# FNet block with SwiGLU, one core: hidden matrices loaded by 64 rows, modulation added up on VectorE, list of steps ranked anew, branch hint at the end

## The chip, the core and the metric

The kernel runs on one core of one Trainium2 chip. The metric is the device time in microseconds of one execution; "the time" of a kernel is the median over runs. A core has TensorE (PE, with its weight loads shown apart as PEld), VectorE (DVE), ScalarE (ACT), GpSimd (POOL) and SyncE (SP). Each engine works through its own list of instructions in the order in which the program issued them. SP issues most transfers, GpSimd those that gather rows or add to what is in memory.

## The reference

```
x    = A_x                                       # [1, 2048, 512]
mod  = (silu(c) @ w_mod) -> sa, ca, ga, sb, cb, gb   # six vectors of 512
h    = layernorm(x) * (1 + ca) + sa
a, b = h @ dft_hid_re.T, h @ dft_hid_im.T        # transform along the 512
y    = dft_seq_re @ a - dft_seq_im @ b           # transform along the 2048
x    = x + ga * y
h    = layernorm(x) * (1 + cb) + sb
x    = x + gb * ((silu(h @ w1) * (h @ w3)) @ w2) # 512 -> 1792 -> 512
```

All is float32. The kernel multiplies most matrices by splitting each into a high part and a low part (three products) in a faster matmul format, and it uses the symmetries of the transform matrices.

## The kernel before, in words

**Stages.** The program has three stages: the hidden transform of the first normalised rows, the sequence transform, and the SwiGLU part. The edits sit in the first stage, in what comes before it, and at the end of the third.

**Before the first stage.** SP issues in this order: `c`; the two halves of x block 0 (`load_x`, L205 and L207); the four blocks of the modulation matrix that give `ca` and `sa` (`load_wm`, L216, 512 KB each; v = 1 is `ca`, v = 0 is `sa`); x block 1; the hidden transform's matrices (`load_hid`, L226, real and imaginary part for each of four column groups dt); x blocks 2 and 3. Meanwhile `keep_warm` runs dummy matmuls (L270), x block 0 is normalised (L424 to L445) and turned by TensorE (L460). Then `mod_sum` multiplies the modulation matrix by silu(c) with matmuls of one column (L292); each (v, h) is a group of 8 matmuls, all in one PSUM bank, and after each group VectorE moves or adds the four columns into `mod1` (L302, L93).

**The first stage.** It goes over NK = 8 blocks k, each of two sides of 128 rows. The steps of a block are: statistics, root, inverse, scale (`stats`, `root`, `inverse`, `scale`), transposes (`turn`), modulation of the turned rows (`mod`, writes `hm`, L476 on ScalarE or L478 on VectorE), sums and differences of the two sides (`sum`, writes `hs`), their high and low parts (`hh`, `hl`), the second side's copy (`h1`), four products with the hidden matrices (`prod`, L524), the odd half (`odd`), the mirrored product (`mirror`, L560), the product with the differences (`diff`, L541), and the copies of the results out of PSUM as high and low parts (`uh`, `us`, `ul`, `up`, `ush`, `ulh`). The hidden matrices themselves are prepared per dt: high part on ScalarE (`wh`), low part on VectorE (`wl`), differences on GpSimd (`wd`, L390, L395), negated copies on ScalarE (`wn`).

**The order.** These steps are tasks with a rank, a list of needs and a planned duration for each engine that can do them. `arrange` keeps a clock for each engine and, again and again, issues among the tasks that could begin within 0.3 us of the earliest the one with the lowest rank. Ranks are offsets from `k * PACE`. The lines with `at(...)` tell the planner at what time the loads and the modulation are supposed to be there. The planner's result is only an order of issue: on the chip an engine waits at the head of its list for whatever that instruction needs.

**After it.** `seq_unit` (L714) begins the sequence transform as soon as the last row block's products are there. In the third stage `down` computes an output block; the last eight `y` in the list are the last eight such blocks.

**The end.** A flag that the kernel computed says whether the general kernel has to run instead. Every engine reads it and branches (L2340).

Of the kernel before, what the change touches and what calls it, by code (L numbers as in the profile page):

```python
# [12 lines left out]
OP = mybir.AluOpType  # L13
# [29 lines left out]
def folded(nc, pools, c, cp, wmr, wmc, x, xt, ctr, cti, wdr, wdi, w1, w3, w2, out):  # L43
# [8 lines left out]
    consts, small, big, psum, dram = pools  # L52
# [169 lines left out]
    def load_hid(dt):  # L222
        i, par = HD[dt]
        raw_w[dt] = take(F32, "w")
        for m, w in enumerate((wdr, wdi)):
            nc.sync.dma_start(raw_w[dt][:, m, :], w[i][par::2].rearrange("r q n -> q r n"))  # L226
# [4 lines left out]
    load_wm(0)  # L231
    load_x(1)
    for dt in range(ND):
        load_hid(dt)
# [51 lines left out]
    mod_acc = bank(6)[:, : 4 * ND].rearrange("p (a b) -> p a b", b=ND)  # L286

    def mod_sum(v, h):

        for dt in range(ND):  # L290
            for n in range(2):
                nc.tensor.matmul(  # L292
                    mod_acc[:, 2 * v + h, dt : dt + 1],
                    hid_cols(wm[v, h][:, n, :], dt),
                    sc[:, 2 * h + n : 2 * h + n + 1],
                    start=n == 0,
                    stop=n == 1,
                )
        give(wm.pop((v, h)))

    def mod_half(v):
        nc.vector.tensor_scalar(mod1[:, v, :], mod_acc[:, 2 * v, :], float(v), None, op0=OP.add)  # L302

    def mod_end(v):
        plus(mod1[:, v, :], mod_acc[:, 2 * v + 1, :], mod1[:, v, :])
# [993 lines left out]
    def last_steps(k):  # L1299
        r = k * PACE  # L1300
        wait = [f"us{k}", f"ul{k}", f"mirror{k}.1", *[f"wd{dt}" for dt in range(ND)]]
        task(f"diff{k}", r + 7, wait, lambda: hid_difference(k), PE=0.96)
        task(f"up{k}", r + 8, [f"diff{k}", f"odd{k}"], lambda: high_columns(k, 0), DVE=0.61)
        task(f"ush{k}", r + 12, [f"up{k}"], lambda: high_columns(k, 1), ACT=0.55)
        task(f"ulh{k}", r + 14, [f"ush{k}"], lambda: high_columns(k, 2), DVE=0.61)

    PACE = 7.5
# [21 lines left out]
    at(12.0, "turn0.0", "turn0.1")  # L1329
    at(13.2, "x1")  # L1330
    for dt in range(ND):
        at(14.5 + 1.6 * dt, f"w{dt}")
    for k in range(2, 4):
        at(21.0 + 1.8 * (k - 2), f"x{k}")
    for engine in clear:
        clear[engine] = 13.2
# [3 lines left out]
    for dt in range(ND):  # L1340
        task(f"wh{dt}", -8 + 2 * dt, [f"w{dt}"], lambda dt=dt: w_highs(dt), ACT=0.8)
        task(f"wl{dt}", -6 + 2 * dt, [f"wh{dt}"], lambda dt=dt: w_lows(dt), DVE=0.8)
        task(f"wd{dt}", -6 + 2 * dt, [f"wl{dt}"], lambda dt=dt: differ_w(dt), POOL=3.0)
# [5 lines left out]
    task("zz", 2 * PACE, [], clear_z, ACT=1.0)  # L1349
    for k in range(NK):  # L1350
        r = k * PACE
        both = [f"{k}.0", f"{k}.1"]
        if k:
            for s in range(2):
                task(
                    f"stats{k}.{s}", r - 13 + s / 2, [f"x{k}"],
                    lambda k=k, s=s: norm_stats(k, s), DVE=0.85,
                )
            task(
                f"root{k}", r - 12.2, [f"stats{n}" for n in both], lambda k=k: norm_root(k), ACT=0.2  # L1360
            )
            task(f"inverse{k}", r - 12, [f"root{k}"], lambda k=k: norm_inverse(k), DVE=0.4)
            free_banks = [f"mod{k - 2}.{dt}" for dt in range(ND)] if k > 1 else []
            for s in range(2):
                task(
                    f"scale{k}.{s}", r - 11.5 + s, [f"inverse{k}"],
                    lambda e, k=k, s=s: norm_scale(k, s, e), ACT=0.63, DVE=0.54,
                )
                task(
                    f"turn{k}.{s}", r - 11 + s, [f"scale{k}.{s}", *free_banks],  # L1370
                    lambda k=k, s=s: turn_rows(k, s), PE=0.5,
                )
        for dt in range(ND):
# [12 lines left out]
        task(f"h1{k}", r - 5, sums_done, lambda k=k: mirror_part(k), ACT=0.55)
        for dt in range(ND):
            needs = [f"hl{k}", f"wl{dt}"]
            if dt == 0 and k > 1:
                needs.append(f"up{k - 2}")  # L1390
            if dt:
                needs.append(f"prod{k}.{dt - 1}")
            if dt == 2:
                needs.append(f"odd{k}")
            task(f"prod{k}.{dt}", r + 2 * dt, needs, lambda k=k, dt=dt: hid_product(k, dt), PE=0.72 + 0.23 * (dt == 0))
        task(f"odd{k}", r + 1, [f"prod{k}.1"], lambda k=k: hid_odd(k), ACT=0.53)
        for n in range(2):
            needs = [f"h1{k}", *[f"wl{dt}" for dt in range(ND)], *[f"wn{dt}" for dt in range(2)]]
            if k:
                needs.append(f"uh{k - 1}.{n}")  # L1400
            if k == NK // 2:
                needs += [f"wd{dt}" for dt in range(ND)]
            if n:
                needs.append(f"mirror{k}.0")
            us_pe = 0.91 if k != NK // 2 else 2.7 + 0.9 * n
            task(f"mirror{k}.{n}", r + 3 + n, needs, lambda k=k, n=n: hid_mirror(k, n), PE=us_pe)
            task(
                f"uh{k}.{n}", r + 4 + n, [f"mirror{k}.{n}", "zz"] if k == NK // 2 else
                [f"mirror{k}.{n}"], lambda k=k, n=n: mirror_highs(k, n), ACT=0.53,
            )  # L1410
        task(f"us{k}", r + 5, [f"prod{k}.3"], lambda k=k: low_columns(k, 0), ACT=0.53)
        task(f"ul{k}", r + 6, [f"us{k}"], lambda k=k: low_columns(k, 1), DVE=0.61)
# [167 lines left out]
    for i in range(len(items)):  # L1580
# [723 lines left out]
def fnet_swiglu_block(  # L2304
# [28 lines left out]
    bad = folded(nc, (*pools, dram), *args)  # L2333
# [6 lines left out]
    with tc.If(flag != 0, preferred_fallthrough_block=False):  # L2340
# [57 lines left out]
```

## Time and profile before

| | us |
|---|---|
| median of 3 runs | 749.0 |
| lowest, highest run | 748.25, 749.11 |
| the profiled execution: its time, its span | 749.39, 747.5 |
| busy in the span: PE, DVE, ACT, POOL | 700.2, 548.8, 426.4, 127.6 |
| first modulated row (L476) begins | 23.40 |
| last load of a hidden matrix used (L87) | 55.87 |
| first matmul of the sequence stage (L714) begins | 123.3 |
| last computing instruction ends | 738.04 |

The profile is one execution. Its page gives the busy time of each engine, the span in 40 slices with each engine's busy tenths, the clock granted to TensorE and the transfer rate, and the chain of work that ended last. Rows in order of time read: start, duration, engine, line, operation, output from inputs, shape, count, and in brackets how long the engine had been idle and what ended it. "SPq" rows are transfers as SP issues them: their duration is the issue, not the landing.

### The profile page before, as it was taken

Reading aid. Unit: us, or ns where it says so; the run is one execution under the profiler, and the core shown is the slowest. Engines: PE = TensorE matmul, PEld = TensorE weight load, DVE = VectorE, ACT = ScalarE, POOL = GpSimd, SP = SyncE. Lnnn points to the kernel's source line nnn. Section 1 sums busy time; section 2 is a strip of 40 time slices with the busy share of each in tenths; the row PEclk is TensorE's granted clock in tenths of the full one; section 3 lists DMA queues with packets and bytes.
Section 4 is the critical chain, followed back from the end, with each engine's and each line's share of the span. In section 5 each row is a group of like instructions: output and inputs, shape, how many; then the busy total and the mean of one; then the engine's idle time right before and its main releaser. Section 6 shows DMA issues by size and latency. Waiting matters only on the chain.

```text
span 747.5 us, 8859 instructions
## 1 busy us (share of the span) xinstructions
PE 700.2 (94%) x3140; PEld 572.2 (77%) x3140; DVE 548.8 (73%) x873; ACT 426.4 (57%) x694; POOL 127.6 (17%) x147
## 2 busy tenths in 40 slices
PE   8618989999999999989999999999999999999994
PEld 5407878888888888868788788777888888888783
DVE  2318887899889997767998888789566655665662
ACT  2208877753554456563667867687655655656430
POOL 1212204634424500010011011001100101001000
PEclk8558999999999999999999999999999999999998
DMA  5142305997859753054186655745947548456503
GB/s 186 51 132 81 114 1 169 347 316 246 284 183 323 248 180 140 28 90 81 57 206 119 181 94 133 142 84 113 232 135 169 118 79 177 69 122 128 155 0 117
DMA packets 37716, 108.92 MB, mean 146 GB/s; under 512 B 4640, under 2 KB 4896, under 8 KB 37664
## 3 DMA queue, kind: packets, MB, share of 16 engines
q0 software_dynamic: 12352, 43.00, 27.9%
q1 hardware_dynamic: 25312, 65.29, 25.9%
q8 instruction: 26, 0.43, 0.2%
q14 instruction: 26, 0.21, 0.1%
HBM read 76.81 MB, written 33.55 MB: 148 GB/s over the span
## 4 chain that ended last, share of the span: by engine, by line
PE 70%; DVE 7%; issue 6%; ACT 6%; SPq 4%; DMA 4%; POOL 0%; POOLq 0%; ACTq 0%; DVEq 0%
PE bank L100 45%; PE bank L714 24%; SPq L226 4%; DMA w<-in_wdi 3%; DMA sum<-y 1%; DVE hm L478 1%; DVE hl L90 1%; ACT xc L858 1%; ACT y L308 1%; ACT hm L476 1%; DVE hs L93 1%; DVE st L424 0%; PE bank L560 0%; POOL sum L1110 0%; DVE ul L90 0%
## 5 line engine op out<-in xcount | busy, mean ns | idle before, releaser
L100 PE MATMUL bank<-hf,w2h 128*128 128x512 f32 (+1 forms) x452 | 140.8, 391 | 0.5 <-ACT y L308 0.2
L1110 POOL DMA_DIRECT2D sum<-y x48 | 41.1, 855 | 390.5 <-ACT y L308 373.0
L100 PEld LDWEIGHTS bank<-hf,w2h 128*128 128x128 f32 x452 | 84.3, 188 | 22.4 <-DVE hf L90 3.5
L100 PE MATMUL bank<-hf,w2l 128*128 128x512 f32 (+1 forms) x226 | 87.6, 388 | 0.0
L308 ACT ACTIVATE y<-bank,gb 128x512 f32<-128x512 f32 x96 | 64.9, 682 | 18.6 <-PE bank L100 18.2
L87 ACT ACTIVATE hf<-v 128x512 fp32r<-128x512 f32 x56 | 35.3, 630 | 67.1 <-DVE v L96 62.5
L93 DVE TENSOR_TENSOR v<-bank,x 128x512 f32<-128x512 f32 x36 | 24.7, 686 | 34.8 <-PE bank L100 34.8
L714 PE MATMUL bank<-d,us 128*128 128x512 f32 x128 | 49.9, 390 | 0.0
L714 PE MATMUL bank<-bh,us 128*128 128x512 f32 x128 | 49.9, 390 | 0.0
L714 PE MATMUL bank<-bh,ul 128*128 128x512 f32 x128 | 49.8, 389 | 0.0
L714 PE MATMUL bank<-l,us 128*128 128x512 f32 x128 | 49.8, 389 | 0.0
L714 PE MATMUL bank<-d,uh 128*128 128x512 f32 x128 | 49.8, 389 | 0.0
L714 PE MATMUL bank<-l,uh 128*128 128x512 f32 x128 | 49.8, 389 | 0.0
L100 PEld LDWEIGHTS bank<-hf,w2l 128*128 128x128 f32 x226 | 42.4, 188 | 8.3
L170 POOL DMA_INDIRECT re<-in_ctr,mirror x32 | 36.4, 1137 | 71.9 <-DVE ul L90 35.8
L93 DVE TENSOR_TENSOR x<-bank,x 128x512 f32<-128x512 f32 x36 | 24.8, 688 | 32.3 <-PE bank L100 28.7
L90 DVE TENSOR_TENSOR hf<-v,hf 128x512 fp32r<-128x512 f32 x56 | 38.5, 687 | 12.2 <-ACT hf L87 12.1
L87 ACT ACTIVATE x<-bank 128x512 f32<-128x512 f32 x72 | 41.4, 586 | 7.2 <-PE bank L100 6.5
L1188 ACT ACTIVATE v<-v 128x512 f32<-128x512 f32 x36 | 22.7, 632 | 39.0 <-DVE v L93 39.0
L170 POOL DMA_INDIRECT im<-in_cti,mirror x32 | 34.3, 1073 | 36.4 <-PE bank L714 10.8
L524 PE MATMUL bank<-wu,hh 128*128 128x256 f32 x128 | 27.1, 306 | 13.7 <-ACT ho L87 10.4
L524 PEld LDWEIGHTS bank<-wu,hh 128*128 128x128 f32 x128 | 22.4, 204 | 17.8 <-ACT ho L87 11.8
(241 smaller groups left out, 1807.8 us busy)
## 6 DMA issues: line engine op xcount, KB each, us to landing
sum<-y POOLq DMA_DIRECT2D x48, 512.0 KB
w<-in_w SPq DMA_DIRECT2D x42, 512.0 KB
re<-in_ctr SPq DMA_DIRECT2D x32, 256.0 KB
im<-in_cti SPq DMA_DIRECT2D x32, 256.0 KB
wmc<-in_wmc SPq DMA_DIRECT2D x8, 512.0 KB
xr<-in_xt SPq DMA_DIRECT2D x8, 512.0 KB
sum<-xr SPq DMA_DIRECT2D x8, 512.0 KB
x<-in_x SPq DMA_DIRECT2D x12, 256.0 KB
```

The source lines that it names most:

```text
L87: nc.scalar.activation(dst, src, AF.Copy, scale=scale)
L90: nc.vector.tensor_tensor(out=dst, in0=a, in1=b, op=OP.subtract)
L93: nc.vector.tensor_tensor(out=dst, in0=a, in1=b, op=OP.add)
L100: nc.tensor.matmul(acc, lhs[a], rhs[b], start=first and n == 0, stop=last and n == len(PASSES) - 1, skip_group_check=more,)
L170: nc.gpsimd.indirect_dma_start(dst, None, rows, bass.IndirectOffsetOnAxis(ap=at, axis=0))
L226: nc.sync.dma_start(raw_w[dt][:, m, :], w[i][par::2].rearrange("r q n -> q r n"))
L308: nc.scalar.activation(dst, src, AF.Identity, scale=by)
L476: nc.scalar.activation(dst, src, AF.Identity, bias=sa, scale=ca1)
L524: nc.tensor.matmul(halves(hb[k])[:, m, :], sides((hh, hl)[a][k])[:, dt, m, :], wu[dt][:, b, m, :], start=False, stop=dt % 2 == 1 and n == ...
L714: nc.tensor.matmul(acc[what, e], lhs, rhs, start=begin and i == 0, stop=(end or (turn and what == "x")) and i == len(terms) - 1, skip_grou ...
L1110: nc.gpsimd.dma_start(sums[t, d // 2], y, accum_op=OP.add)
L1188: behind(k != 0 or q == 0, lambda: nc.scalar.activation(v, src, AF.Silu))
```

## The change

1. **Loads.** `load_hid` issued one transfer for a matrix's part, with the destination's 128 partitions written as 2 groups of 64. Now it issues one for each group: 16 transfers of 128 KB and not 8 of 256 KB. The first column group's are issued ahead of x block 1.
2. **Modulation.** For each v, ScalarE scales one block by silu(c), VectorE adds the other three onto it (each multiplied by its own column of silu(c)), and TensorE sums over partitions with 4 matmuls for each v: 8 and not 32. There are two `keep_warm` matmuls between the two groups and one after them. `zz` is cleared here and no longer in the list.
3. **List.** Ranks stand in a table, `PACE` is 7.15 and not 7.5, the planner's times for the loads and some planned durations are others.
4. **End.** The branch is laid out without a preferred block, and each engine gets a hint ahead of the fourth last output block that the branch is likely taken.

```diff
-            nc.sync.dma_start(raw_w[dt][:, m, :], w[i][par::2].rearrange("r q n -> q r n"))
+            for q in range(2):
+                nc.sync.dma_start(raw_w[dt][q * 64 : (q + 1) * 64, m, :], w[i][par::2, q])
...
     load_wm(0)
+    load_hid(0)
     load_x(1)
-    for dt in range(ND):
+    for dt in range(1, ND):
         load_hid(dt)
...
-    mod_acc = bank(6)[:, : 4 * ND].rearrange("p (a b) -> p a b", b=ND)
-    def mod_sum(v, h):
+    mod_acc = bank(6)
+    def mod_scale(v, h):
+        w, own = wm[v, 0][:, 0, :], wm[v, h]
+        if h == 0:
+            copy_by(w, w, sc[:, 0:1])
+        for n in range(1 - h, 2):
+            nc.vector.scalar_tensor_tensor(
+                w, own[:, n, :], sc[:, 2 * h + n : 2 * h + n + 1], w, op0=OP.mult, op1=OP.add
+            )
+    def mod_sum(v):
         for dt in range(ND):
-            for n in range(2):
-                nc.tensor.matmul(
-                    mod_acc[:, 2 * v + h, dt : dt + 1],
-                    hid_cols(wm[v, h][:, n, :], dt),
-                    sc[:, 2 * h + n : 2 * h + n + 1],
-                    start=n == 0,
-                    stop=n == 1,
-                )
...
+            nc.tensor.matmul(
+                mod_acc[:, v * ND + dt : v * ND + dt + 1],
+                hid_cols(wm[v, 0][:, 0, :], dt),
+                onesf[:, :1],
+                start=True,
+                stop=True,
+            )
+        nc.vector.tensor_scalar(
+            mod1[:, v, :], mod_acc[:, v * ND : (v + 1) * ND], float(v), None, op0=OP.add
+        )
...
-    PACE = 7.5
+    PACE = 7.15
+    RANK = {
+        "stats": -17, "root": -15, "inverse": -12, "scale": -11.5, "turn": -11,
+        "mod": -7, "sum": -11.5, "hh": -6.5, "hl": -9.7, "h1": -5,
+        "prod": -2, "odd": -3, "mirror": 3, "uh": 4, "us": 5, "ul": 6,
+        "diff": 3.4, "up": 6, "ush": 12, "ulh": 6.6,
+    }   # before: -13, -12.2, -12, -11.5, -11, -9, -8, -6.5, -6, -5, 0, 1, 3, 4, 5, 6, 7, 8, 12, 14
...
-    for v in (1, 0):
-        mod_sum(v, 0)
-        mod_half(v)
-        mod_sum(v, 1)
-        mod_end(v)
-    keep_warm(2)
-    give(first_tmp)
     nc.gpsimd.memset(flat(zero), 0.0)
     copy(nought, zero[:, 0, :P])
-    at(13.2, "mod")
+    for v in (1, 0):
+        for h in range(2):
+            mod_scale(v, h)
+    clear_z()
+    for v in (1, 0):
+        mod_sum(v)
+        keep_warm(2 if v else 1)
+    give(first_tmp)
+    at(13.6, "mod")
     at(12.0, "turn0.0", "turn0.1")
-    at(13.2, "x1")
+    at(14.0, "x1")
     for dt in range(ND):
-        at(14.5 + 1.6 * dt, f"w{dt}")
+        at((12.1, 16.0, 18.0, 20.0)[dt], f"w{dt}")
     for k in range(2, 4):
-        at(21.0 + 1.8 * (k - 2), f"x{k}")
+        at(22.0 + 2.0 * (k - 2), f"x{k}")
...
-    task("zz", 2 * PACE, [], clear_z, ACT=1.0)
...
             if at == "y":
+                if (i, len(seconds)) == (len(items) - 1, 4):
+                    tc.mark_branch_hint_location("general", hint="LikelyTaken")
                 down(*seconds.popleft())
...
-    with tc.If(flag != 0, preferred_fallthrough_block=False):
+    with tc.If(flag != 0, label="general"):
         general(nc, pools, *args)
```

More of the change, by code (lines that the diff above doesn't have):

```diff
@@ L43, in folded @@
 def folded(nc, pools, c, cp, wmr, wmc, x, xt, ctr, cti, wdr, wdi, w1, w3, w2, out):
-    consts, small, big, psum, dram = pools
+    consts, small, big, psum, dram, tc = pools
     free = deque(range(SLOTS))
@@ L1301, in last_steps @@
         wait = [f"us{k}", f"ul{k}", f"mirror{k}.1", *[f"wd{dt}" for dt in range(ND)]]
[L1302 to L1305, printed above, removed]
-    PACE = 7.5
+        task(f"diff{k}", r + RANK["diff"], wait, lambda: hid_difference(k), PE=0.96)
+        task(f"up{k}", r + RANK["up"], [f"diff{k}", f"odd{k}"], lambda: high_columns(k, 0), DVE=0.61)
+        task(f"ush{k}", r + RANK["ush"], [f"up{k}"], lambda: high_columns(k, 1), ACT=0.55)
+        task(f"ulh{k}", r + RANK["ulh"], [f"ush{k}"], lambda: high_columns(k, 2), DVE=0.61)
+    PACE = 7.15
+    RANK = {
+        "stats": -17,
+        "root": -15,
+        "inverse": -12,
+        "scale": -11.5,
+        "turn": -11,
+        "mod": -7,
+        "sum": -11.5,
+        "hh": -6.5,
+        "hl": -9.7,
+        "h1": -5,
+        "prod": -2,
+        "odd": -3,
+        "mirror": 3,
+        "uh": 4,
+        "us": 5,
+        "ul": 6,
+        "diff": 3.4,
+        "up": 6,
+        "ush": 12,
+        "ulh": 6.6,
+    }
     seq_steps = []
@@ L1316, in folded @@
         turn_rows(0, side)
[L1317 to L1323 removed]
     nc.gpsimd.memset(flat(zero), 0.0)
     copy(nought, zero[:, 0, :P])
[L1328 removed]
+    for v in (1, 0):
+        for h in range(2):
+            mod_scale(v, h)
[5 more added lines that the diff above has]
+    at(13.6, "mod")
     at(12.0, "turn0.0", "turn0.1")
[L1330 removed]
+    at(14.0, "x1")
     for dt in range(ND):
[L1332 removed]
+        at((12.1, 16.0, 18.0, 20.0)[dt], f"w{dt}")
     for k in range(2, 4):
[L1334 removed]
+        at(22.0 + 2.0 * (k - 2), f"x{k}")
     for engine in clear:
[L1336 removed]
+        clear[engine] = 13.6
     for k in range(4, NK):
@@ L1359, in folded @@
             task(
-                f"root{k}", r - 12.2, [f"stats{n}" for n in both], lambda k=k: norm_root(k), ACT=0.2
+                f"root{k}", r + RANK["root"], [f"stats{n}" for n in both], lambda k=k: norm_root(k), ACT=0.2
             )
-            task(f"inverse{k}", r - 12, [f"root{k}"], lambda k=k: norm_inverse(k), DVE=0.4)
+            task(f"inverse{k}", r + RANK["inverse"], [f"root{k}"], lambda k=k: norm_inverse(k), DVE=0.4)
             free_banks = [f"mod{k - 2}.{dt}" for dt in range(ND)] if k > 1 else []
@@ L1365, in folded @@
                 task(
-                    f"scale{k}.{s}", r - 11.5 + s, [f"inverse{k}"],
-                    lambda e, k=k, s=s: norm_scale(k, s, e), ACT=0.63, DVE=0.54,
+                    f"scale{k}.{s}", r + RANK["scale"] + s, [f"inverse{k}"],
+                    lambda e, k=k, s=s: norm_scale(k, s, e), ACT=0.63, DVE=0.46,
                 )
                 task(
-                    f"turn{k}.{s}", r - 11 + s, [f"scale{k}.{s}", *free_banks],
+                    f"turn{k}.{s}", r + RANK["turn"] + s, [f"scale{k}.{s}", *free_banks],
                     lambda k=k, s=s: turn_rows(k, s), PE=0.5,
@@ L1374, in folded @@
             task(
-                f"mod{k}.{dt}", r - 9 + 0.1 * dt, ["mod", *[f"turn{n}" for n in both]],
-                lambda e, k=k, dt=dt: modulate_rows(k, dt, e), ACT=0.36, DVE=0.36,
+                f"mod{k}.{dt}", r + RANK["mod"] + 0.1 * dt, ["mod", *[f"turn{n}" for n in both]],
+                lambda e, k=k, dt=dt: modulate_rows(k, dt, e), ACT=0.45, DVE=0.43,
             )
@@ L1379, in folded @@
             task(
-                f"sum{k}.{m}", r - 8 + m, [f"mod{k}.{dt}" for dt in range(ND)],
+                f"sum{k}.{m}", r + RANK["sum"] + m, [f"mod{k}.{dt}" for dt in range(ND)],
                 lambda k=k, m=m: mirror_sums(k, m), DVE=0.61,
@@ L1383, in folded @@
         sums_done = [f"sum{n}" for n in both]
-        task(f"hh{k}", r - 6.5, sums_done, lambda k=k: sum_highs(k), ACT=0.97)
-        task(f"hl{k}", r - 6, [f"hh{k}"], lambda k=k: sum_lows(k), DVE=1.16)
-        task(f"h1{k}", r - 5, sums_done, lambda k=k: mirror_part(k), ACT=0.55)
+        task(f"hh{k}", r + RANK["hh"], sums_done, lambda k=k: sum_highs(k), ACT=0.97)
+        task(f"hl{k}", r + RANK["hl"], [f"hh{k}"], lambda k=k: sum_lows(k), DVE=1.16)
+        task(f"h1{k}", r + RANK["h1"], sums_done, lambda k=k: mirror_part(k), ACT=0.55)
         for dt in range(ND):
@@ L2332, in fnet_swiglu_block @@
     args = c, cp, wmr, wmc, x, xt, ctr, cti, wdr, wdi, w1, w3, w2, out
-    bad = folded(nc, (*pools, dram), *args)
+    bad = folded(nc, (*pools, dram, tc), *args)
     flag = nc.values_load(
```

23 lines of the change are left out of this document (9 added, 14 removed).

## The prediction, made before the changed kernel had run

> **What bounds the kernel now.** I read the page's slices first, then the table of busy time by windows, then the instructions in order of time for the first 65 us, then the DMA answers. The first four rows are from the page (forty slices of 18.7 us), the rest from the window table, whose columns are the length, the busy time of PE, PEld, DVE, ACT and POOL, the granted clock, the DMA engines' share and GB/s.
>
> ```profile
> span 747.5 us, 8859 instructions
> PE   8618989999999999989999999999999999999994
> PEclk8558999999999999999999999999999999999998
> DMA  5142305997859753054186655745947548456503
> ...
> 11.00:12.00 1.00, 0.74 (x7) 0.66 (x7) 0.16 (x1) 0.00 (x0) 0.00 (x0) 0.96 1.03 397
> 12.00:13.00 1.00, 1.00 (x5) 1.00 (x6) 0.00 (x0) 0.00 (x0) 0.00 (x0) 0.50 0.29 111
> 23.90:58.20 34.30, 9.84 (x27) 5.91 (x26) 8.58 (x19) 8.24 (x18) 7.82 (x9) 0.50 0.31 101
> 58.20:123.30 65.10, 60.74 (x375) 53.00 (x375) 59.35 (x112) 52.58 (x102) 12.02 (x11) 0.96 0.21 67
> 123.30:738.10 614.80, 609.69 (x2664) 497.62 (x2662) 476.52 (x726) 360.97 (x570) 103.36 (x110) 1.00 0.60 158
> ```
>
> From 123.3 us on TensorE is busy 609.69 of 614.80 us: there the change edits nothing but the end. The time that can move lies before. From 23.9 to 58.2 no engine has even 10 us of work, and from 58.2 to 123.3 VectorE (59.35 of 65.10) and TensorE (60.74) are both nearly full. The instructions in order of time, and the DMA answer for 15 to 45 us, name what the empty stretch waits for:
>
> ```profile
> 14.48 5.09 SPq L226 DMA_DIRECT2D w<-in_wdi  x1
> ...
> 35.03 3.61 SPq L226 DMA_DIRECT2D w<-in_wdi  x1
> 55.87 0.42 ACT L87 ACTIVATE wu<-w 128x256 fp32r<-128x256 f32 x1 [5.60 <-DMA w<-in_wdi]
> 57.62 1.01 ACT L476 ACTIVATE hm<-bank,mod 128x256 f32<-128x256 f32 x2
> ...
> DMA packets 750, 1.53 MB, mean 51 GB/s; under 512 B 12, under 2 KB 12, under 8 KB 749
> q1 hardware_dynamic: 749, 1.51, 13.1%
> ```
>
> The eight transfers of the hidden matrices go one behind the other on SP's queue at 51 GB/s and 13.1% of 16 engines, which is two engines. The last lands at 55.87 us, and ScalarE, which has its work in order, can't begin the second row block (57.62) before it.
>
> **The loads.** The chunk in question is 8 transfers of 256 KB (2.10 MB), written as [2, 64, 512]; they become 16 of 128 KB written as [64, 512]. The x transfers begin with a dimension of 64 too ([64, 2, 512]), and they and the modulation matrices came like this:
>
> ```profile
> 7.00:9.40 2.40, 1.79 (x8) 0.73 (x7) 1.09 (x5) 1.31 (x3) 0.00 (x0) 1.00 1.03 420
> 9.40:10.70 1.30, 1.30 (x14) 1.30 (x13) 0.00 (x0) 0.00 (x0) 0.00 (x0) 1.00 1.00 408
> ...
> DMA packets 1253, 3.08 MB, mean 257 GB/s; under 512 B 260, under 2 KB 260, under 8 KB 1253
> ...
> 4.72 0.69 SPq L205 DMA_DIRECT2D x<-in_x  x1
> ```
>
> The third row is for 0 to 12 us. First come x0 (0.52 MB) and four blocks of 0.52 MB, 2.62 MB in all; 3.08 MB by 12.0 us at 0.41 MB/us put their end at 10.9 us. I take the x rate for the new form. Then w0 lands 1.3 us later, at 12.2; x1, which now stands behind w0, at 13.5 (it is not needed before the modulation is done, below); w1 to w3, 1.57 MB, at 17.3. SP's issue doesn't hold this up by much: w0 is issued from 4.7 us on, and 16 issues and x1's two at 0.7 us each end at 17.3 us. The transfers of x2 and x3 stand behind all of w, as before. So w3 lands at about 18 where it was 55.9.
>
> [...]
>
> **The modulation.** Before, each of four pieces is 8 matmuls (16 records), and the next waits for the addition by VectorE:
>
> ```profile
> 8.01 0.81 ACT L443 ACTIVATE x<-x,rs 128x512 f32<-128x512 f32 x1 [0.43 <-DVE rs L435]
> 8.73 0.29 ACT L87 ACTIVATE nought<-zero 128x128 fp32r<-128x128 f32 x1
> 9.74 1.94 PE L292 MATMUL bank<-sc,wmr 128*128 128x1 f32 x16
> 11.94 3.57 PE L292 MATMUL bank<-sc,wmr 128*128 128x1 f32 x16 [0.26 <-DVE mod L302]
> 23.02 3.76 PE L270 MATMUL bank<-tmp 128*128 128x512 f32 x4
> 23.20 0.16 DVE L93 TENSOR_TENSOR mod<-bank,mod 128x4 f32<-128x4 f32 x1 [3.67 <-PE bank L292]
> 23.40 1.02 ACT L476 ACTIVATE hm<-bank,mod 128x256 f32<-128x256 f32 x2 [14.38 <-DVE mod L93]
> 25.03 0.69 DVE L93 TENSOR_TENSOR hs<-hm 128x512 f32<-128x512 f32 x1
> 25.64 0.68 DVE L90 TENSOR_TENSOR hs<-hm 128x512 f32<-128x512 f32 x1
> ```
>
> The matmuls take 1.94 us at clock 1.00 and 3.57 at 0.50. After: two scalings on ScalarE (nearest row 0.81 us; the first begins when the copy to `nought` ends at 9.02 and is done by 9.7), six additions of 128x512 on VectorE (no row; nearest are the sums, begun 0.61 us apart), and two groups of 4 matmuls. VectorE adds from 9.7 to 13.4; the first three are done at 11.6. The first group is half of 3.57 us, as the clock falls to 0.50 at 12 us, and ends at 13.4. Behind it on TensorE stand two `keep_warm` matmuls, 3.76 us by the row above, to 17.2, and only then the second group, to 19.0; 0.2 us for VectorE's last addition: the first modulated row starts at 19.2 instead of 23.4. At clock 1.00 for both groups it would be 17.5; 19.2 is nearest to the rows, since the clock was 0.50 from 12 us. The `keep_warm` pair is thus the new wait: VectorE's and ScalarE's lists begin with modulated rows, so that everything behind is held to 19.2. That also hides w0 to w3 (18), and the clearing of `z`, which moves into ScalarE's idle time before it.
>
> **From there to the sequence stage.** The first matmul of the sequence stage came at 123.3 us. VectorE is the fullest engine of the stage and its work in it is what stands in the table: 8.58 + 59.35 = 67.9 us. This has to be done from 19.2 on. The idle time beside it in the dense part was 65.10 - 59.35 = 5.75 us, and I keep that: 19.2 + 67.9 + 5.75 = 92.9, against 123.3, which is 30.4 us less. A check by TensorE: its work is 60.74 us plus 18 of the 24 products of the first row block and a transpose that it did earlier; from about 23 us with 5 us of ramp and gaps this also ends near 92. So no engine but these two matters.
>
> **The ranks.** They remove no instruction. The ends are 5.75 us gained (no idle time left in the dense part) and 5.75 lost (twice as much). The sums and low parts move nearer to their inputs, the statistics four ranks earlier and x has long landed; against it, the additions of GpSimd now fall beside a busy VectorE: such a one took 1.17 us and not 0.73, and VectorE's low part beside one 0.60 and not 0.42:
>
> ```profile
> 27.38 0.42 DVE L374 SCALAR_TENSOR_TENSOR wu<-w,wu 128x256 fp32r<-128x256 f32 x1
> 28.35 1.17 POOL L390 TENSOR_TENSOR wd<-w 128x256 fp32r<-128x256 f32 x1 [3.53 <-DMA w<-in_wdr]
> 33.56 0.73 POOL L390 TENSOR_TENSOR w<-w 128x256 f32<-128x256 f32 x1 [4.05 <-DMA w<-in_wdi]
> 33.97 0.60 DVE L374 SCALAR_TENSOR_TENSOR wu<-w,wu 128x256 fp32r<-128x256 f32 x1 [3.89 <-ACT wu L87]
> ```
>
> Ten such additions at up to 0.2 us cost VectorE up to 2 us. I take 1.5 us gained in all, near the middle.
>
> **The end.** The last store leaves VectorE at 738.04 and its data are in by 740.7. After that only instruction blocks move (the last computing instruction; the rates from 738.5 to 741 us in forty slices; then those from 741 to 747.5, and the two queues):
>
> ```profile
> 737.56 0.48 DVE L1101 SCALAR_TENSOR_TENSOR xr<-bank,gb,xr 128x256 f32<-128x256 f32 x1 [0.63 <-PE bank L100]
> ...
> GB/s 17 0 0 0 0 262 115 246 360 311 344 344 181 66 0 0 0 0 0 0 0 131 0 16 0 16 16 0 16 0 16 16 16 16 0 0 0 0 0 0
> ...
> GB/s 0 0 0 0 0 0 101 50 50 0 0 0 0 0 0 0 0 0 0 0 0 0 0 50 0 0 0 0 0 0 0 0 0 0 0 0 0 0 50 0
> DMA packets 5, 0.05 MB, mean 8 GB/s; under 512 B 0, under 2 KB 0, under 8 KB 0
> q14 instruction: 4, 0.03, 1.8%
> q8 instruction: 1, 0.02, 0.9%
> ```
>
> They come at 742.0, 744.7 and 747.2: rounds 2.6 us apart. A hint four output blocks from the end can spare such a round, and the layout that is no longer asked for can add one. Ends: 5.4 us gained (742.0 to 747.5) and 2.6 lost. I take 1 us gained, as most of these blocks may lie behind the kernel's own branch, which no row tells.
>
> **Sum.** -30.4 - 1.5 - 1.0 = -33 us on the profiled execution (749.39 us, span 747.5), which stands 0.4 above the median of 749.0 (748.25 to 749.11). So 749.0 - 33 = 716.
>
> **Rivals.** *Half rate.* A transfer to 64 partitions may move at half the 410 GB/s; no row has one that small across. Then w0 lands at 13.5, x1 at 14.8 and w3 at 10.9 + 2.6 + 1.3 + 7.7 = 22.5. Mirror products and the last quarter of the first products want w3; they come after the low parts of the first rows, 4 us behind 19.2, so up to 1.5 us of it would show: 717.5. [...]
>
> *The change doesn't do what it says.* If the new form still runs on two engines, 2.10 MB at 51 GB/s take 41 us from 12.2 and w3 lands at 53.4, 2.5 us earlier than now: 745.5 with the end. For it speaks nothing but that SP's queue is the same; the x rows speak against.
>
> *Slower.* If a transfer of one half ran on one engine, at 25.6 GB/s, the sixteen would take 82 us, to 94 us, 38 later than 55.9: 787. It decides below 48 GB/s (2.10 MB in 55.9 - 12.2 us). For it: now one engine may well carry each half. Against: the x transfers also lead with 64 and reached 420 GB/s.
>
> *The list turns out badly,* with clock 0.50 long into the dense part or twice the idle time: 716 + 7 = 723. In the trace the clock was back within 5 us of dense work:
>
> ```profile
> 62.00:63.00 1.00, 1.00 (x4) 0.81 (x4) 0.96 (x4) 0.96 (x3) 0.02 (x1) 0.50 0.65 209
> 63.00:64.00 1.00, 1.00 (x7) 0.82 (x6) 1.00 (x2) 1.00 (x3) 0.00 (x0) 0.94 0.58 205
> ```
>
> **How the numbers follow.** Forecast 0.50, half rate 0.35, a bad list 0.10, two engines still 0.03, one engine 0.02. Predicted 716. The range reaches down to the earliest start (17.5), the full gain of the ranks (4 more) and most of the end's (4 more): 706; up to the bad list: 723. The last two cases stay outside. A difference of 0.2% (1.5 us) is about what can be told here. All cases but the last two are far faster; two engines would be 3.5 us faster by this sum, with its end in doubt: faster 0.96, same 0.02, slower 0.02.
>
> **What would show it.** DMA near 100% of 16 engines (or 50%, half rate) from 10.9 until 18 (22.5); no SP transfer of 5 us; the first `hm` at 19.2, behind the `keep_warm` pair; VectorE with about 68 us of work from there; first sequence matmul at about 91; from it to the end 623 us, with one round of instruction blocks fewer. I am wrong if the second group of matmuls isn't held, if the dense stage takes other than 72 us, or if the sequence stage then waits for its own loads.

## The result, and the profile after

The changed kernel took 717.5 us (median of 4 runs, 715.58 to 718.29), the kernel before 749.06 beside it (748.25 to 751.49): a ratio of 0.957, 95% interval 0.9541 to 0.9599. The prediction was 716.0, its range 706 to 723. The profiled execution took 717.52 us, its span is 715.7.

From the page of the kernel after (slices of 17.9 us now):

```profile
span 715.7 us, 8791 instructions
PE   7699999999999999999999999999999999999995
DVE  4889887999899977679997887897666456664663
PEclk8599999999999999999999999999999999999998
DMA  8630089878588530442667566376854748447503
```

and from its window table, with the columns named in the prediction:

```profile
18.80:93.08 74.28, 66.68 (x398) 57.82 (x398) 66.34 (x126) 60.64 (x120) 18.43 (x18) 0.88 0.29 92
93.08:708.02 614.94, 609.40 (x2664) 497.78 (x2662) 477.21 (x728) 360.82 (x569) 104.80 (x110) 1.00 0.60 158
12.00:17.00 5.00, 5.00 (x14) 2.93 (x14) 2.00 (x4) 1.25 (x3) 2.77 (x3) 0.52 1.05 246
```

The slices with TensorE at 1 and 8 tenths have gone from the PE row. The window rows are the stretch from the first modulated row to the first sequence matmul, from there to the end of the last computing instruction, and five microseconds of the loads. The long stretch is what it was (614.94 us, before 614.72). The span splits into four pieces:

| | before | after | difference |
|---|---|---|---|
| first modulated row begins | 23.40 | 18.80 | -4.60 |
| from there to the first sequence matmul | 99.92 | 74.28 | -25.64 |
| from there to the last computing instruction's end | 614.72 | 614.94 | +0.22 |
| from there to the span's end | 9.46 | 7.68 | -1.78 |
| span | 747.5 | 715.7 | -31.8 |

The third window row also answers the loads' open question. The DMA engines are full (1.05), and yet they move only 246 GB/s, where the x and modulation loads had 408 to 420 before. What that did is read from the issues of the last hidden matrix, from the window row of the last three microseconds of these loads, and from the answer on the tile `w` for the very last transfer (issued at 19.73 us):

```profile
19.09 1.24 SPq L227 DMA_DIRECT2D w<-in_wdi  x2
...
18.50:21.50 3.00, 2.41 (x4) 0.74 (x3) 2.79 (x7) 1.99 (x6) 2.82 (x5) 0.50 0.63 194
...
DMA to landing us min/median/max: 3.6/3.6/3.6
```

The last hidden matrix lands at 23.3 us (19.73 + 3.6), not at 18 (full rate) but near the 22.5 of the half-rate rival. At the end the engines are no longer full (0.63): SP issues without a pause one transfer of 128 KB in about 0.64 us, which is 205 GB/s, and the row has 194. So the rate of 246 GB/s sets the first part of these loads and SP's issue the last. The instructions in order of time of VectorE and TensorE show the modulation:

```profile
11.68 0.75 DVE L296 SCALAR_TENSOR_TENSOR wmr<-wmr,sc 128x512 f32<-128x512 f32 x1
11.82 1.62 PE L303 MATMUL bank<-tmp,wmr 128*128 128x1 f32 x8 [2.11 <-DVE wmr L296]
...
13.22 1.54 DVE L296 SCALAR_TENSOR_TENSOR wmr<-wmr,sc,wmr 128x512 f32<-128x512 f32 x2 [0.79 <-DMA wmr<-in_wmr]
13.30 3.76 PE L272 MATMUL bank<-tmp 128*128 128x512 f32 x4
...
16.86 1.71 PE L303 MATMUL bank<-tmp,wmr 128*128 128x1 f32 x8
...
18.60 0.16 DVE L310 TENSOR_SCALAR mod<-bank 128x4 f32<-128x4 f32 x1 [3.77 <-PE bank L303]
18.80 0.54 DVE L487 TENSOR_SCALAR hm<-bank,mod 128x256 f32<-128x256 f32 x1
...
93.08 0.40 PE L723 MATMUL bank<-bh,us 128*128 128x512 f32 x1
```

As forecast, the `keep_warm` pair (L272, 13.30 to 17.06) stands between the two groups of modulation matmuls (L303), and the first `hm` follows the second group. The last block of the modulation arrives later than forecast: the additions at 13.22 had waited 0.79 us for a DMA.

### The profile page after: what moved, and what is told of

It reads as the page before. It is cut to its first block, busy times and chain, and to the rows that moved or that the text cites. A ratio compares the mean times of both kernels' runs of the same rounds, so it can differ in the third digit from the quotient of the medians.

```text
span 715.7 us, 8791 instructions
## 1 busy us (share of the span) xinstructions
PE 689.8 (96%) x3094; PEld 563.4 (79%) x3094; DVE 551.9 (77%) x873; ACT 428.7 (60%) x700; POOL 129.8 (18%) x147
## 4 chain that ended last, share of the span: by engine, by line
PE 60%; issue 23%; DVE 6%; DMA 4%; ACT 4%; POOL 2%; SPq 1%; POOLq 0%; ACTq 0%; DVEq 0%
PE bank L100 32%; PE bank L723 25%; POOL sum L1119 2%; PE bank L533 2%; DMA sum<-y 2%; DMA x<-in_x 1%; PE bank L569 1%; DMA wmr<-in_wmr 1%; DVE hl L90 1%; ACT hm L485 1%; PE bank L469 1%; DVE hs L90 1%; ACT y L317 0%; DVE hm L487 0%; ACT ho L87 0%
## 5 line engine op out<-in xcount | busy, mean ns | idle before, releaser
L93 DVE TENSOR_TENSOR v<-bank,x 128x512 f32<-128x512 f32 x36 | 24.7, 686 | 34.8 <-PE bank L100 34.8
L93 DVE TENSOR_TENSOR x<-bank,x 128x512 f32<-128x512 f32 x36 | 24.8, 688 | 32.4 <-PE bank L100 28.7
L90 DVE TENSOR_TENSOR hf<-v,hf 128x512 fp32r<-128x512 f32 x56 | 38.5, 687 | 12.2 <-ACT hf L87 12.1
L100 PE MATMUL bank<-h2h,w1h 128*128 128x512 f32 x80 | 31.8, 397 | 1.5 <-ACT h2h L87 1.5
L100 PE MATMUL bank<-h2l,w1h 128*128 128x512 f32 x80 | 32.0, 400 | 0.8 <-DVE h2l L90 0.8
```

Source lines behind the costliest of these rows:

```text
L90: nc.vector.tensor_tensor(out=dst, in0=a, in1=b, op=OP.subtract)
L93: nc.vector.tensor_tensor(out=dst, in0=a, in1=b, op=OP.add)
L100: nc.tensor.matmul(acc, lhs[a], rhs[b], start=first and n == 0, stop=last and n == len(PASSES) - 1, skip_group_check=more,)
```

## The experiments

My theory was that the loads carry nearly all of the gain, at half rate, and that modulation, ranks and hint are worth a few microseconds each; the rival, that much of it comes from the parts beside the loads. Further questions were what the lower rate, the `keep_warm` pair and GpSimd's additions cost. The kernels ran in three groups, each on one chip with the kernel before beside it (749.71, 749.86 and 749.17 us): e1 to e4, e5 to e8, e9 to e11. "hm" is when the first modulated row begins, "seq" the first sequence matmul, "tail" the time from the last computing instruction's end to the span's end; the columns to "tail" are from the profiled execution.

| | hm | seq | stage between | tail | median (range) of 5 (e1, e2: of 4) | ratio to before, 95% |
|---|---|---|---|---|---|---|
| e1 loads only | 22.32 | 97.61 | 75.29 | 10.06 | 724.39 (723.01 to 725.42) | 0.9661, 0.963 to 0.9691 |
| e2 loads undone | 18.43 | 119.09 | 100.66 | 7.32 | 743.28 (742.52 to 743.83) | 0.9913, 0.9883 to 0.9943 |
| e3 no pair between | 17.09 | 91.28 | 74.19 | 7.70 | 715.02 (713.24 to 716.03) | 0.9535, 0.9509 to 0.9562 |
| e4 128 partitions | 19.13 | 90.86 | 71.73 | 7.08 | 712.96 (711.69 to 713.62) | 0.9504, 0.9479 to 0.9528 |
| e5 after again | 17.48 | 91.02 | 73.54 | 7.68 | 715.26 (714.26 to 717.59) | 0.9545, 0.9524 to 0.9567 |
| e6 e3 and e4 | 16.96 | 89.14 | 72.18 | 7.30 | 711.74 (710.98 to 713.43) | 0.9498, 0.9479 to 0.9516 |
| e7 old ranks | 17.91 | 93.57 | 75.66 | 7.53 | 718.19 (715.01 to 718.82) | 0.9564, 0.9539 to 0.959 |
| e8 old end | 17.52 | 91.36 | 73.84 | 10.10 | 717.76 (716.6 to 720.34) | 0.9586, 0.9563 to 0.9609 |
| e9 fewer GpSimd additions | 18.14 | 91.28 | 73.14 | 7.77 | 713.37 (711.39 to 716.5) | 0.9527, 0.9501 to 0.9554 |
| e10 old modulation | 23.26 | 95.83 | 72.57 | 7.78 | 716.48 (715.08 to 719.95) | 0.9572, 0.9547 to 0.9598 |
| e11 after, third time | 18.65 | 92.14 | 73.49 | 7.84 | 716.67 (715.41 to 717.66) | 0.9568, 0.9549 to 0.9586 |

The columns say more than the medians where these differ by under 2 us: the long stretch, from the first sequence matmul to the last computing instruction, took 613.4 to 613.9 us in the profiles of e3, e4, e6 and e8, and 614.4 to 615.3 in the others. TensorE's clock tells them apart: in the others it falls once in this stretch, for 3.41 us (in after at 305.70 us, in the kernel before at 336.18), where no edit reaches.

### The loads alone, and all but the loads (e1, e2)

e1 is the kernel before with one line replaced; e2 is the kernel after with the reverse:

```diff
-            nc.sync.dma_start(raw_w[dt][:, m, :], w[i][par::2].rearrange("r q n -> q r n"))
+            for q in range(2):
+                nc.sync.dma_start(raw_w[dt][q * 64 : (q + 1) * 64, m, :], w[i][par::2, q])
```

> The kernel before with the 64-row transfers alone; order of loads, modulation, list and end are the old ones. Theory A (the loads carry most of the gain, and once they are early the modulation sets the start of the first stage): the first modulated row stays at 23.4 us, the last hidden matrix lands at about 22, and the stage takes the 74 to 76 us that it takes in the changed kernel, so that the first sequence matmul comes at 97 to 99 and the time is 723 to 725. Rival B (the loads carry all of it, modulation and list nothing): 719, which is the changed kernel's 717.5 and the 1.8 us of its end. Rival C (the new list is what makes the early loads useful): over 727.

> The changed kernel with the old transfers of [2, 64, 512]. Theory A: they run at 51 GB/s again, the last lands at 53 to 56 us, the first sequence matmul comes at 121 to 124, and the time is 745 to 748: without the loads the other edits are worth only what the end gives (1.8 us) and at most 2.5 us of an earlier last load. Rival B (the rest of the change has a gain of its own in the first stage): under 743.

The loads alone gave 25.3 of the 31.6 us (749.71 to 724.39). The other three parts alone gave 6.4 (749.71 to 743.28), and the two add up to 31.7, so that little of it is shared. e1 came as theory A had it, but for an earlier first modulated row; e2 lies between its two theories, and both its stage and its end are earlier than A had them. In order of time, e1's first modulated row, which still waits for the modulation's last addition (`mod`, L93) as before:

```profile
22.32 1.02 ACT L477 ACTIVATE hm<-bank,mod 128x256 f32<-128x256 f32 x2 [13.31 <-DVE mod L93]
```

and of e2 the last additions of the modulation, the first modulated row and the last hidden matrix:

```profile
12.38 1.54 DVE L295 SCALAR_TENSOR_TENSOR wmr<-wmr,sc,wmr 128x512 f32<-128x512 f32 x2
...
18.43 0.54 DVE L486 TENSOR_SCALAR hm<-bank,mod 128x256 f32<-128x256 f32 x1
...
56.21 0.42 ACT L87 ACTIVATE wu<-w 128x256 fp32r<-128x256 f32 x1 [5.51 <-DMA w<-in_wdi]
```

In e2 the matrices are as late as ever (56.21 us, before 55.87). The modulation, 5 us earlier, buys nothing there, but from that point to the sequence stage it takes 62.88 us and the kernel before 67.45 (123.32 - 55.87). These 4.6 us are put down to the new list only by argument: in e2 the clock was also back earlier behind the last matrix (61.8 us, before 63.1). The tail gives the other 2.1.

### 128 partitions at a time (e4)

The hidden matrices come from a second copy whose layout allows one transfer of 256 KB to all 128 partitions:

```diff
-            for q in range(2):
-                nc.sync.dma_start(raw_w[dt][q * 64 : (q + 1) * 64, m, :], w[i][par::2, q])
+            nc.sync.dma_start(raw_w[dt][:, m, :], w[i, par])   # w: (hdr, hdi), copies laid out [i, par, partition, n]
```

> The changed kernel with each hidden matrix's part loaded by one transfer to all 128 partitions with a leading dimension of 128, from a second copy of the matrix laid out for it: 8 transfers of 256 KB and not 16 of 128 KB. Theory A (64-row transfers run at half rate because of their width): the rate between 11 and 17 us is about 410 GB/s and not 240, the last matrix lands at about 17.5 and the last block of the modulation at about 11 and not 13.2. As the dummy matmuls still hold the modulation to 18.8, the time falls by 0 to 1 us. Rival B (the rate is set by SP's issue of 0.6 us a transfer): the same, as the transfers are half as many, but then SP would never wait in the changed kernel, where it waited 5 us. Rival C (the late w hold the stage): the time falls by 2 to 4 us.

In the window table of e4, with the columns as before:

```profile
12.00:17.00 5.00, 4.79 (x12) 2.91 (x13) 2.83 (x5) 2.09 (x4) 3.30 (x4) 0.56 1.05 390
```

and in its instructions:

```profile
22.69 0.41 DVE L90 TENSOR_TENSOR wu<-w,wu 128x256 fp32r<-128x256 f32 x1
```

The same five microseconds and the same busy share of the engines, but 390 GB/s and not 246. e4 also has fewer and larger transfers and another order of the rows in memory. The DMA answers for 12 to 17 us, of after and then of e4, tell these apart:

```profile
DMA packets 720, 1.23 MB, mean 246 GB/s; under 512 B 119, under 2 KB 119, under 8 KB 720
q1 hardware_dynamic: 720, 1.23, 105.0%
...
DMA packets 1068, 1.95 MB, mean 390 GB/s; under 512 B 121, under 2 KB 121, under 8 KB 1068
q1 hardware_dynamic: 1068, 1.95, 105.2%
```

Without the small packets, after's engines are busy for 84 us (1.05 of 16 engines for 5 us) with 601 packets, about 0.14 us each, and e4's with 947, about 0.09 each, though nearly all are rows of 2 KB in both. In the kernel before, where one transfer wrote both halves from the same rows in memory, one took about 0.085 us (13.1% of 16 engines, 30 us, 738 packets). So it is the single row that takes longer, not the gaps between transfers, and the kernel before, with the same order in memory, doesn't have it: the lower rate (246 and not 390 GB/s) goes with writing 64 partitions at a time. VectorE's first low part of a matrix (`wu`) takes 0.41 us here and 0.94 in after; e9 below takes this up. Ratios of 0.9504 (0.9479 to 0.9528) here and 0.9545 (0.9524 to 0.9567) for e5 overlap by 0.0004; the stage is 1.8 us shorter than e5's and 2.5 than after's. So the rate is theory A's, but the gain is rival C's: 246 and not 390 GB/s cost about 2 us (e6 beside e3, below, is the cleaner pair).

### The pair between the groups (e3), and both together (e6)

e3 puts the `keep_warm` matmuls behind both groups; e6 has this and e4's loads:

```diff
     for v in (1, 0):
         mod_sum(v)
-        keep_warm(2 if v else 1)
+    keep_warm(3)
```

> The changed kernel with the two dummy matmuls taken from between the two groups of the modulation's matmuls; all three stand behind the second group. Theory A (the pair holds the second group, and with it the whole stage): the first modulated row starts at about 16.9 us and not 18.8, since VectorE's last addition ends at 14.8 and the group takes 1.7; the time falls by 1.5 to 2 us to about 715.7. Rival B (the loads of w, which land until 21.7, hold the stage): the row starts earlier, but the time stays within 0.5 us of 717.5. Rival C (the pair keeps the clock up): the clock comes back later than 36 us and the time rises.

> Both of the earlier edits on the changed kernel: full-width loads of the hidden matrices, and no dummy matmuls between the groups of the modulation. Alone, the loads took the first sequence matmul from 93.1 to about 90.9 us, the dummy matmuls to 91.3. Theory A (two waits one behind the other: the modulation holds the start, the contention and the late matrices the next 8 us; the gains add): the first modulated row at about 17.1, the first sequence matmul at 88.5 to 89.5, the time 4 to 5.5 us below the changed kernel. Rival B (the same wait seen twice): 90.5 to 91, and 2 to 3 us below.

The second group and the first modulated row of e3:

```profile
14.98 1.87 PE L303 MATMUL bank<-tmp,wmr 128*128 128x1 f32 x8 [1.85 <-DVE mod L310]
...
17.09 0.54 DVE L487 TENSOR_SCALAR hm<-bank,mod 128x256 f32<-128x256 f32 x1
```

Against after's profile the row begins 1.7 us earlier and the sequence stage 1.8 us earlier. Against e5, whose first group had the full clock, it is 0.4 earlier and the sequence stage 0.26 later, and the medians (715.02 and 715.26) can't be told apart. The pair holds the second group in both, but costs the start little (0.4 us) where the clock falls late. e6 is the best kernel run: 711.74 us, 89.14 us to the sequence stage, 1.9 ahead of e5, 3.0 ahead of e11. Its rows are theory A's; its median is 3.5 below e5's, between A's 4 and B's 3. From e4 alone (712.96) its median isn't clearly apart.

e6 and e3 differ in the loads alone, begin the stage together and have the clock at 0.50 for as long (6.8 and 3.4 us). Of e3, and then of e6, VectorE's first low part of a matrix and the low part `hl` of the first sums:

```profile
21.18 0.96 DVE L90 TENSOR_TENSOR wu<-w,wu 128x256 fp32r<-128x256 f32 x1
24.67 1.23 DVE L90 TENSOR_TENSOR hl<-hs,hh 128x1024 fp32r<-128x1024 f32 x1
...
21.43 0.41 DVE L90 TENSOR_TENSOR wu<-w,wu 128x256 fp32r<-128x256 f32 x1
22.78 1.21 DVE L90 TENSOR_TENSOR hl<-hs,hh 128x1024 fp32r<-128x1024 f32 x1
```

Four low parts stand ahead of `hl`. They take about 0.95 us each in e3, where GpSimd's last four additions run from 21.14 to 24.47, and 0.41 in e6, where these are over at 20.96. `hl` begins 1.9 us earlier in e6, and the first sequence matmul 2.1.

### The same kernel again (e5, e11)

> The changed kernel itself once more, as the measure for the three that run beside it on this chip: 715.5 to 718.5.

> The changed kernel itself, as the measure for the two beside it: 715 to 718. With the clock falling at 12 to 13 us the first modulated row comes at 18.8, with a later fall at 17.5; the first sequence matmul at 93 or 91.

Three times the same program: 715.26, 716.67 and 717.5 us, the first sequence matmul at 91.02, 92.14 and 93.08. The clock differs. From the window tables, after's rows first:

```profile
12.00:13.00 1.00, 1.00 (x7) 1.00 (x7) 0.43 (x1) 0.41 (x1) 0.00 (x0) 0.58 1.07 256
32.00:36.00 4.00, 4.00 (x19) 3.81 (x18) 3.81 (x10) 4.00 (x7) 0.00 (x0) 0.50 0.08 26
36.00:40.00 4.00, 4.00 (x25) 3.54 (x24) 2.48 (x4) 3.12 (x8) 0.00 (x0) 0.99 0.00 0
```

and those of e5:

```profile
12.00:13.00 1.00, 1.00 (x9) 1.00 (x10) 0.90 (x2) 0.08 (x1) 0.00 (x0) 1.00 1.05 244
13.00:14.00 1.00, 1.00 (x2) 0.41 (x2) 0.96 (x3) 0.42 (x1) 0.59 (x1) 0.63 1.08 219
16.00:17.00 1.00, 1.00 (x9) 1.00 (x7) 0.00 (x0) 0.00 (x0) 0.38 (x1) 0.66 1.05 256
20.00:21.00 1.00, 0.00 (x0) 0.00 (x0) 1.00 (x2) 0.58 (x2) 1.00 (x3) 0.54 0.74 221
30.00:31.00 1.00, 0.49 (x4) 0.49 (x5) 0.00 (x0) 1.00 (x4) 0.00 (x0) 0.84 1.00 385
```

A row's mean clock tells when it changed between 1.00 and 0.50: in after it falls at 12.2 us, in e5 at 13.3. So e5's first group of modulation matmuls still has the full clock; it has it again from 16.7 to 20.1, which takes in part of the second group, and its first `hm` starts at 17.48. In e5 the clock is back for the rest of the stage at 30.3 us, in after only at 36: from 32 to 36 TensorE is busy all the time and issues 19 matmul records, in the next 4 us at full clock 25. Some 2 us between two executions, and so part of any small difference here, come from this. From after to e5 the fall moved by 1.1 us and the return by almost 6. In the clock records of the two kernels the changes lie whole multiples of 3.41 us apart (in after at 12.15, 36.05, 305.70 and 309.11 us, in before at 11.92, 63.12, 336.18 and 339.60), and the rows of e5 fit this (13.3, 16.7, 20.1 and 30.3).

### The old ranks (e7), the old end (e8)

e7 gives every task its old rank and `PACE` its 7.5, while the planner's times and durations stay new; e8 has the branch without the hint and with its old layout:

```diff
-    with tc.If(flag != 0, label="general"):
+    with tc.If(flag != 0, preferred_fallthrough_block=False):
...
-                if (i, len(seconds)) == (len(items) - 1, 4):
-                    tc.mark_branch_hint_location("general", hint="LikelyTaken")
```

> The changed kernel with PACE 7.5 and the old ranks; loads, modulation, planned times and end stay changed. Theory A (the list is worth 1 to 1.5 us, as predicted): the first modulated row stays at 18.8 us, the first sequence matmul comes at 94 to 95, the time is 1 to 1.5 us above the changed kernel. Rival B (the list is worth nothing or is worse): equal or below. Rival C (the list is what fills the stage): over 3 us above.

> The changed kernel with the old end: no hint, and the branch laid out with the preferred block. Theory A (the hint spares one of the rounds of instruction blocks): from the last computing instruction to the end of the span 9.5 us and not 7.7, three rounds of instruction blocks and not two; the time 1.8 us above the changed kernel. Rival B (the difference of 1.8 us was chance): the same time within 0.5 us.

With the old ranks the stage is 2.1 us longer than e5's and the median 2.9 higher, though the intervals overlap; between executions of like mean clock (0.983 or 0.984: 718.19, 715.48 and 715.01 against 714.26 and 715.58 without the old ranks) it is about 1, from few runs that overlap. The list is worth 1 to 3 us here, which doesn't tell theory A from C. e7's profile also shows a way that isn't idle time: the planner gave VectorE 18 of the `hm` instructions and not 11 as in e5 (8.7 and 5.8 us), so that its work in the stage is 70.10 us and not 66.65; and the clock was lower in the stage (a mean of 0.91, in e5 0.93). Which of the two made the 2.1 us is not shown. In e8 the tail is 10.10 and not 7.68 us and the median 2.5 higher, as theory A had it. The transfer rates of after from the last computing instruction to the end, in forty slices of 0.19 us:

```profile
GB/s 320 320 54 91 112 336 192 0 43 11 48 11 16 0 0 0 0 0 0 0 85 43 43 0 0 0 0 0 0 0 0 0 0 0 0 43 0 0 0 0
```

and those of e8, in slices of 0.25 us:

```profile
GB/s 333 207 0 154 308 89 32 0 0 8 8 12 4 0 0 0 32 65 32 0 0 0 0 0 0 0 0 32 0 0 0 0 0 0 0 0 32 0 0 0
```

After the store's data, after has groups in the 21st and the 36th slice (2.9 us apart), e8 in the 17th, the 28th and the 37th (2.8 and 2.3 us): three rounds of instruction blocks with the old end, two with the new. e8 undoes the hint and the layout together and doesn't tell which of them spared the round.

### Fewer additions on GpSimd (e9), the old modulation (e10)

e9 leaves out four of GpSimd's ten operations on the hidden matrices and fills their tiles; e10 has the 32 matmuls of the modulation in four pieces, as before.

```diff
-            pool(dd[:, 0, :], r[:, 0, 1, :], r[:, 0, 0, :], OP.subtract)
-            pool(dd[:, 1, :], r[:, 1, 0, :], r[:, 1, 1, :], OP.subtract)
+            for m in range(2):
+                nc.gpsimd.memset(dd[:, m, :].bitcast(F32), 0.0)
```

> The changed kernel with four of GpSimd's ten additions on the hidden matrices (those of the last two column groups, which ran from 20.5 to 24.4 us) left out: a fill with zeros of the same size takes their place, so that GpSimd reads nothing there. Loads, modulation and list are the same. Theory A (these additions slow VectorE's two-input instructions beside them): the second sum takes 0.69 us and not 1.2, the low parts 0.42 and not 0.95, VectorE is ahead by 1.7 to 2.1 us at 25 us, and the first sequence matmul comes 1 to 2 us earlier than in the changed kernel, near the 90.9 of the full-width loads, whose gain was then this. Rival B (the full-width loads gained because the last matrices were there earlier): the durations fall, but the first sequence matmul stays within 0.5 us of the changed kernel's on this chip.

> The changed kernel with the old modulation: four groups of 8 matmuls with VectorE between them, one pair of dummy matmuls behind; loads, list and end stay changed. Theory A (the modulation sets the start of the stage and the stage follows it): the first modulated row at 22.3 to 23.5 us, the first sequence matmul 3 to 5 us later than in the changed kernel, the time 3 to 5 us above it. Rival B (the last matrices, here by 21.7, hold the stage anyway): up to 1 us above.

VectorE's and GpSimd's instructions at the start of the stage, of after:

```profile
20.52 3.86 POOL L399 TENSOR_TENSOR wd<-w 128x256 fp32r<-128x256 f32 x4
...
21.72 1.21 DVE L90 TENSOR_TENSOR hs<-hm 128x512 f32<-128x512 f32 x1
22.85 0.94 DVE L90 TENSOR_TENSOR wu<-w,wu 128x256 fp32r<-128x256 f32 x1
23.72 0.94 DVE L383 SCALAR_TENSOR_TENSOR wu<-w,wu 128x256 fp32r<-128x256 f32 x1
```

and of e9:

```profile
22.14 1.06 POOL L407 MEMSET wd<- 128x256 f32 x4
22.21 0.41 DVE L90 TENSOR_TENSOR wu<-w,wu 128x256 fp32r<-128x256 f32 x1
```

Beside GpSimd's additions VectorE's two-input operations take 0.94 us and not 0.41; beside its fills they don't get longer. e9's stage is 73.14 us, e11's on the same chip 73.49, and its first sequence matmul comes 0.86 us earlier, between its two theories. That is small because e11's additions had mostly ended before the low parts: one of the four took 0.94 there, the others 0.41 to 0.43. VectorE reaches `hl` at 23.55 us in e9 and at 24.44 in e11, and these 0.89 us are what the sequence stage gains. e9's median is 3.3 lower than e11's, of which the clock has a part: at 0.98 e9 had 716.5 and the kernel after 717.49 and, as e5, 716.0.

e10 begins its first modulated row at 23.26 us and reaches the sequence stage at 95.83, 3.7 later than e11, and yet its median (716.48) is e11's (716.67). Its five executions fall apart by the clock: 719.95 and 719.81 at a mean of 0.974 to 0.976, 715.08 to 716.48 at 0.983 to 0.984. The profiled one is the first of these. So its stage came as theory A had it and its median as rival B, and the modulation's gain is 0 to 3 us; that this depends on the clock is read from five executions.

## Why the prediction was right, and where its steps were not

**Where the time is.** Right. The gain lies ahead of the sequence stage (-30.24 of -31.8 us) and 25.3 us of it come with one line of the loads.

**Loads.** The step that failed is "I take the x rate for the new form". The form does reach all engines (share 1.05), but at 246 GB/s, and with 128 partitions 390. This was the half-rate rival, with 0.35 against 0.50. Its landing was near (22.5; measured 23.3), though it left out SP's issue, and its time came out (717.5; measured 717.5). That the time agrees to the tenth is luck, as its path did not: it let products wait for w3, but in the stage no compute engine but GpSimd waits for a hidden matrix (in after the last such wait, 1.01 us, ends at 18.08). The late matrices cost 2 us and not 1.5, by way of GpSimd: its additions come later and fall beside VectorE's low parts. So "no engine but these two matters" failed too, and the price of such a meeting, "up to 0.2 us" from 0.60 for 0.42, was too small: after has 0.94 for 0.41. The half of 410 GB/s, from which that rival was worked out, was my estimate, and no run shows it: 64 partitions at a time, one half and the other in turn, moved 246 GB/s in after and 256 in e1.

**Modulation.** The mechanism was right, the new wait included. The sizes: the last block came at 13.2 and not by 10.9, because w0, issued behind it, shares the engines with it, where the step "w0 lands 1.3 us later" took them one after the other: in e2, whose w0 runs on two engines, the rate falls from 360 to 69 GB/s between 10 and 11 us, so that the block was in by then, and the last additions begin at 12.38 without a wait. An addition took 0.75 us and not 0.61. Both stayed hidden behind the `keep_warm` pair, which ended at 17.06 where 17.2 was forecast, so that `hm` came at 18.80 (19.2 forecast). The end named for clock 1.00, 17.5, is what e5 had, with the full clock in its first group and part of the second.

**The stage.** 72.2 us were forecast (67.9 of work, 5.75 idle, 1.5 less for the ranks), 74.28 measured: 66.34 of work and 7.94 idle. By the prediction's own sign ("other than 72 us") this step failed, and the term that was too small is the idle time. From the window table of after:

```profile
24.00:28.00 4.00, 2.26 (x9) 1.97 (x10) 3.93 (x10) 3.31 (x8) 3.22 (x4) 0.50 0.93 271
28.00:32.00 4.00, 3.31 (x15) 3.02 (x14) 2.24 (x7) 2.00 (x6) 1.77 (x2) 0.50 1.00 362
40.00:93.00 53.00, 50.92 (x335) 44.96 (x334) 48.68 (x91) 44.79 (x90) 8.37 (x7) 1.00 0.19 56
```

With the row for 36 to 40 us above, VectorE idled 1.76 us from 28 to 32, 1.52 from 36 to 40 and 4.32 from 40 to 93: 7.6 of the 7.94. The last is the size of the idle time that I had kept; the first two come on top, at the start of the stage. What the first waits for is read in the instructions of TensorE, ScalarE and VectorE in order of time:

```profile
30.33 0.41 PE L533 MATMUL bank<-wu,hl 128*128 128x256 f32 x1
30.78 0.60 ACT L87 ACTIVATE ho<-bank 128x512 f32<-128x512 f32 x1 [1.14 <-PE bank L533]
31.28 0.56 ACT L485 ACTIVATE hm<-bank,mod 128x256 f32<-128x256 f32 x1
31.73 0.29 ACT L438 ACTIVATE rs<-mv,eps 128x2 f32<-128x2 f32 x1
...
32.05 0.17 DVE L443 RECIPROCAL rs<-rs 128x2 f32<-128x2 f32 x1 [1.74 <-ACT rs L438]
```

VectorE wants the root of the next statistics (`rs`), which ScalarE holds in its list behind a copy `ho`, and that waits for products of TensorE (L533) at half clock. In e5 the same wait is 1.75 us, and in e6 1.44; what follows from 36 to 40 is 0.54 us in e5 (its row for that stretch has 3.46 us of work), whose clock had come back before 32. The rival of the bad list had a part in this. "In the trace the clock was back within 5 us of dense work" did not hold: TensorE was busy 3.31 of 4 us from 28 and got its clock at 36, 8 us later.

**Ranks.** 1.5 us forecast, 1 to 3 by e7.

**The end.** 1 us forecast; 1.78 in the two profiles, 2.4 by e8 (10.10 to 7.68). A round of instruction blocks was spared, as the prediction allowed, and nearly all of its 2.6 us was gained: the choice of 1 us near the middle of its ends was too low.

**Sum.** -30.4 - 1.5 - 1.0 = -33 forecast, -31.8 measured: the first two terms together -31.9 against -30.24, the end -1.0 against -1.78.

**Where the lower rate's 2 us go.** In the runs with the new ranks and early loads, the time from the start of `hl` to the first sequence matmul hardly varies: 66.4 to 66.8 us in e3, e4, e5, e6 and e8, where the clock was back by 30.4 us, and 67.7 to 67.9 in after, e9, e10 and e11, where it came back between 34 and 39. So what VectorE loses ahead of `hl` beside GpSimd's additions reaches the sequence stage in full, and a late return of the clock goes with about 1.1 us more. This is a comparison of nine profiles: e9, which takes four of the additions away, fits it, but no run moves them alone.

**Open.** What sets the time at which the clock returns.

## What to carry to other kernels

A transfer's share of the DMA engines and its rate are two readings: here the 13.1% of the engines at 51 GB/s became a share of 0.99 at 256 GB/s with transfers that lead with 64 and not with 2 (e1), and full engines at 246 GB/s became 390 with 128 partitions written at a time (e4). Where a stage begins while TensorE's clock is low, run the unchanged kernel more than once and compare its stages before crediting 2 us to an edit. Undo each part by itself: the four parts here (loads, modulation, list, end) were worth 25, 0 to 3, 1 to 3 and about 2 us, which one comparison of before and after doesn't tell.

## What the runs showed of the hardware that I had not expected

- Transfers of 128 KB to 64 partitions, one half and the other in turn, moved 246 GB/s with the DMA engines' share at 1.05 (after); transfers of 256 KB to 128 partitions 390 GB/s at the same share (e4).
- Rows of 2 KB took a DMA engine about 0.14 us each where 64 partitions were written at a time (after), and about 0.09 where all 128 were (e4).
- TensorE's clock fell at 12.2 us in one profiled execution of the same program and at 13.3 in another, and came back for the rest of the stage at 36.0 and at 30.3 us (after, e5); the changes in the records of before and after lie whole multiples of 3.41 us apart.
- VectorE's two-input operation of 128x256 took 0.41 us alone (e4) or beside GpSimd's fills (e9), and 0.94 beside GpSimd's additions (after); four such in a row went with a sequence stage that began 2.1 us later (e3 beside e6).
- Transfers that were issued later delayed an earlier one: with w0's 64-row transfers behind it the last modulation block was in use at 12.34 to 13.22 us in the three profiles of after, and with w0 on two engines it was in by about 11.
- With the new end (hint and layout) the span ended 7.1 to 7.8 us after the last computing instruction, with the old one 9.5 to 10.1.
